# Top-k attention with a low-rank mixer: another order inside the deep steps

## The chip, the cores and the metric

The kernel runs on one core of one Trainium2 chip. What is measured is the device time of one execution in microseconds, from the first to the last instruction of the core. The core has five engines that run side by side and wait for one another by semaphores: PE (TensorE, the matrix multiplier, with its weight loads as PEld), DVE (VectorE), ACT (ScalarE), POOL (GpSimd) and SP (SyncE, which here only issues DMA).

## What is computed

Eight batches of eight heads; 576 rows of 64 channels in each head; all in fp32. Each row of the attention keeps the 32 largest of its 576 scores. The result goes through a mixer along the sequence (rank 32) and an MLP of 512 to 2048 to 512 channels.

```python
def _attn_ref(q, k, v):                      # q, k, v: (8, 8, 576, 64)
    scores = scale * np.matmul(q, k.transpose(0, 1, 3, 2))
    kth = np.partition(scores, -32, axis=-1)[..., -32:-31]
    scores = np.where(scores >= kth, scores, -1e9)
    attn = np.exp(scores - np.max(scores, axis=-1, keepdims=True))
    attn = attn / (np.sum(attn, axis=-1, keepdims=True) + 1e-09)
    return np.matmul(attn, v)

def _moe_ref(x, U, V, w_ch1, w_ch2):         # x: (8, 576, 512)
    h = x.transpose(0, 2, 1) @ U @ V
    u = x + h.transpose(0, 2, 1)
    return u + np.maximum(u @ w_ch1, 0.0) @ w_ch2
```

## The kernel before

Heads are worked on in pairs, 32 pairs `g` in all. A pair has five steps `t`: four with 128 query rows of both heads, and a tail (`t == NT == 4`) with the last 64 rows of each head, side by side in the partitions. Steps are numbered `n = 5 g + t`. The pieces of a step are these.

```python
def scores(g, t):            # PE: 4 fp32 products of 288 columns; ACT: copies to Ssb
    ...
def front(g, t):             # a generator; each next() issues one part
    ...
    for c in order:
        ms[c] = first[:, c]
        nc.vector.max(ms[c], curs[c])            # the first 8 of the 32
    yield
    for i in range(1, TOPK // 8):
        if i == 1:                               # ACT: exp of head 0
            nc.scalar.mul(nmax[:, 0:n], first[:, 0:n, 0], -SCALE)
            ... weigh(chunks[c], Es[c], nmax[:, c : c + 1])
        for c in order: ... nc.vector.match_replace(nxt, ms[c], curs[c], NEG)
        for c in order: ... nc.vector.max(ms[c], curs[c])
        yield
    if pooled:                                   # head 1: masked by POOL
        nc.gpsimd.tensor_scalar(Es[1], chunks[1], ms[1][:, 7:8], NEG, ALU.is_lt, ALU.mult)
        nc.gpsimd.tensor_tensor(chunks[1], chunks[1], Es[1], ALU.add)
    for c in ...: nc.vector.scalar_tensor_tensor(out=Es[c], ...)   # head 0: masked by DVE
    yield
    if pooled:                                   # ACT: exp of head 1, after POOL
        weigh(chunks[1], Es[1], nmax[:, 1:2], sums[1])
    yield

def turns(g, t):             # a generator: E transposed by PE, copied to PT by ACT
    for h in range(nh):      # nh = 2, in the tail 1
        ... 4 transposes; nc.scalar.copy(PT[...], tp)
        yield
    ... 1 transpose (the last columns); nc.scalar.copy
    yield

def values(g, t):            # PE: PT times v
    ...
    if t == NT:
        inverse(g, ...)      # DVE: 1 / (sum + 1e-9) of the whole pair
        ... 5 fp32 products
        nc.scalar.mul(x[half(h), NT, half(h)], O[half(h), half(h)], den[half(h), 2 * NT :])
        return
    ... 9 fp32 products; nc.scalar.copy(XTs[g][:, cols(t)], O)

def mixed(g, wait):          # a generator, advanced by one at each fill()
    ... 4 transposes of XT; nc.scalar.copy(X4, tp4)
    nc.gpsimd.tensor_tensor(X4, X4, den4, ALU.mult)
    for _ in range(wait): yield
    ... 5 products with U; nc.scalar.copy(Tb, pT); yield
    ... two products with V, x added by PE; copies to uT; two yields
    if gi == NPAIR - 1: fillers.append(mlp(b))   # the batch is complete: its MLP may start
```

`mlp(b)` is a generator too: 256 fp32 products of 320 and then 256 of 256 columns, one per `next`, with the relu on ACT and, at the end of an output block, an addition on POOL and a transposition by PE (`turned_back`). `fill()` puts a fixed share of it between the pieces of attention:

```python
SLOTS, SHORT, EARLY = 8, 0.65, 0.91
share = MLP_WORK / (NPAIR * SLOTS * (NT + SHORT))
def fill(k=1):
    ...
    if mixing and next(mixing[0], True): mixing.pop(0)
    due += share * (SHORT if t == NT else 1) * (EARLY if n <= 2 * ALONE + 2 else 1)
    while due > 0: ... due -= next(fillers[0], None)
```

The first batch (`n < ALONE == 20`) has no MLP beside it and an order of its own. From step 21 on, the deep steps, each step issues the pieces in this order:

```python
fill()
next(turning, None)              # E of step n-2, head 1
fill()
next(turning, None)              # E of step n-2, last columns
fill()
next(ready, None)                # transposes of the next pair's q, k
fill()
if n - 2 >= ALONE:
    values(*divmod(n - 2, CH))
if n + 1 < STEPS:
    scores(*divmod(n + 1, CH))
next(here, None)                 # here is front(n): exp of head 0, second 8
next_params(1)                   # decodes a slab of weights while there are any
if n - 2 >= ALONE and (n - 2) % CH == NT:
    mixing.append(mixed((n - 2) // CH, 4))
fill()
next(here, None)                 # third 8
fill()
if n <= STEPS:
    turning = turns(*divmod(n - 1, CH))
next(turning, None)              # E of step n-1, head 0
fill()
next(here, None)                 # fourth 8
next(last, None)                 # last is front(n-1): exp of head 1
if t in (1, 3):
    next_params(1)
next(here, None)                 # masking
fill()
```

Of the kernel before, what the change touches and what calls it, by code (L numbers as in the profile page):

```python
# [24 lines left out]
def kernel(  # L25
# [35 lines left out]
    NT, TAIL = 4, 64  # L61
# [53 lines left out]
    def rows(t):  # L115
        return P if t < NT else TAIL

    def cols(t):
        return slice(t * P, t * P + rows(t))
# [4 lines left out]
    def half(h):  # L124
        return slice(h * D, (h + 1) * D)
# [139 lines left out]
    def scores(g, t):  # L265


        qkT = qkTs[g]
        n = rows(t)
        S2 = attn.tile([P, 2 * (S + TAIL)], F32, tag="Ssb", name="Ssb", bufs=3)  # L270
        scs = [ps_s.tile([P, 2, 512], F32, tag="sc", name="sc") for _ in range(2)]
        for i, sc in enumerate(scs):
            for h in range(2):
                nc.tensor.matmul(  # L274
                    sc[slice(0, n) if t < NT else half(h), h, 0:HALF],
                    lhsT=qkT[half(h), 0, cols(t)],
                    rhs=qkT[half(h), 1, i * HALF : (i + 1) * HALF],
                    start=True,
                    stop=True,
                )  # L280
        if t == NT:
            for i, sc in enumerate(scs):
                for h in range(2):
                    nc.scalar.copy(
                        S2[half(h), i * HALF : (i + 1) * HALF], sc[half(h), h, 0:HALF]
                    )
            S2s[g, t] = [S2[:, 0:S]]
            return

        main = S2.rearrange("p (h n) -> p h n", h=2)  # L290
        last = S2[:, MAIN : MAIN + 2 * TAIL].rearrange("p (h n) -> p h n", h=2)
        copy = nc.vector.tensor_copy if g + t == 0 else nc.scalar.copy
        copy(main[:, :, 0:HALF], scs[0][:, :, 0:HALF])  # L293
        nc.scalar.copy(main[:, :, HALF:MAIN], scs[1][:, :, 0 : MAIN - HALF])
        nc.scalar.copy(last, scs[1][:, :, MAIN - HALF : HALF])  # L295
        S2s[g, t] = [S2[:, 0:S], S2[:, S : 2 * S]]
# [59 lines left out]
    def turns(g, t):  # L356


        E2 = probs.pop((g, t))
        nh = 2 if t < NT else 1  # L360
        PT = attn.tile([P, 2 * NT + 1, P], F32, tag="PT", name="PT")
        PTs[g, t] = PT
        for h in range(nh):
            tp = ps_t.tile([P, NT, P], F32, tag="tp", name="tp")
            for j in range(NT):
                a = h * (S + TAIL) + j * P
                nc.tensor.transpose(tp[:, j, :], E2[:, a : a + P], ident)  # L367
            nc.scalar.copy(PT[:, NT * h : NT * h + NT], tp)  # L368
            yield
        tp = ps_t.tile([P, P], F32, tag="tp", name="tp")  # L370
        a = MAIN if nh == 2 else S - P
        nc.tensor.transpose(tp, E2[:, a : a + P], ident)  # L372
        nc.scalar.copy(PT[:, NT * nh], tp)
        yield
# [6 lines left out]
    def values(g, t):  # L381

        PT = PTs.pop((g, t))
        va, vd, vt = (a[g % NV] for a in (vas, vds, vts))
        O = ps_t.tile([P, P], F32, tag="tp", name="O")
        if t == NT:
            den, x = dens[g], xs[g % 2]
            inverse(g, 2 * NT if g == NPAIR - 1 else 0, 2 * NT + 1)
            for j in range(NT + 1):
                nc.tensor.matmul(  # L390
                    O,
                    lhsT=PT[:, j],
                    rhs=va[:, :, j, :] if j < NT else vt,
                    start=(j == 0),
                    stop=(j == NT),
                )
            for h in range(2):
                nc.scalar.mul(x[half(h), NT, half(h)], O[half(h), half(h)], den[half(h), 2 * NT :])
            return
        nc.tensor.matmul(O, lhsT=vd, rhs=PT[:, 2 * NT], start=True, stop=False)  # L400
        for j in range(NT):
            for h in range(2):
                nc.tensor.matmul(  # L403
                    O[half(h)],
                    lhsT=va[:, h, j, :],
                    rhs=PT[:, NT * h + j],
                    start=False,
                    stop=(j == NT - 1),
                )
        if t == 0:  # L410
            XTs[g] = attn.tile([P, MAIN], F32, tag="XT", name="XT")
        nc.scalar.copy(XTs[g][:, cols(t)], O)  # L412
# [124 lines left out]
    CH = NT + 1  # L537
    STEPS = NP * CH
    ALONE = NPAIR * CH


    SLOTS, SHORT, EARLY = 8, 0.65, 0.91
    share = MLP_WORK / (NPAIR * SLOTS * (NT + SHORT))
    fillers, mixing, due = [], [], 0.0

    def fill(k=1):

        nonlocal due
        for _ in range(k):
            if mixing and next(mixing[0], True):  # L550
                mixing.pop(0)
            due += share * (SHORT if t == NT else 1) * (EARLY if n <= 2 * ALONE + 2 else 1)
            while due > 0:
                if not fillers:
                    due = 0.0
                    break
                done = next(fillers[0], None)
                if done is None:
                    fillers.pop(0)
                else:  # L560
                    due -= done
# [3 lines left out]
    t = 0  # L565
# [3 lines left out]
    turning = ready = iter(())  # L569
    fronts = {}  # L570
    for n in range(STEPS + 2):
        g, t = divmod(n, CH)
        if n < STEPS:
            if t == 0 and g + 1 < NP:
                load(g + 1)
            if t == 1 and g + 1 < NP:
                ready = prep(g + 1)
            fronts[n] = front(g, t)
            next(fronts[n])
        here, last = fronts.get(n, iter(())), fronts.pop(n - 1, iter(()))  # L580
        if n >= ALONE - 1 and n <= ALONE:

            list(turning)
            if n < ALONE:
                scores(*divmod(n + 1, CH))
            list(turns(*divmod(n - 1, CH)))
            if n < ALONE:
                values(*divmod(n - 2, CH))
                next(here)
            values(*divmod(n - 1, CH))  # L590
            if n < ALONE:
                inverse(g, 0, 2 * NT)
                next(here)
                mixing.append(mixed(g, 1))
                fill()
                next(here)
                next(here)
                continue
            fill()
            scores(*divmod(n + 1, CH))  # L600
            next(here)
            while mixing:
# [3 lines that stand above are left out]
            next(last, None)  # L606
            next(here)
            fill()
            next(here)
            next(here)  # L610
            fill()
            continue
        if n < ALONE:
            next(turning, None)
            next(turning, None)
            scores(*divmod(n + 1, CH))
            fill()
            if n >= 1:
                turning = turns(*divmod(n - 1, CH))
            if n >= 2:  # L620
                values(*divmod(n - 2, CH))
            next(here)
            next_params(1)
            next(turning, None)
            fill()
            next(last, None)
            next(ready, None)
            next(here)
            fill()
            if n >= 2 and (n - 2) % CH == NT:  # L630
                mixing.append(mixed((n - 2) // CH, 3))
            next(here)
            if t == 1:
                next_params(1)
            next(here)
            fill()
            continue
        fill()
        next(turning, None)
        fill()  # L640
        next(turning, None)
        fill()
        next(ready, None)
        fill()
        if n - 2 >= ALONE:
            values(*divmod(n - 2, CH))
        if n + 1 < STEPS:
            scores(*divmod(n + 1, CH))
        next(here, None)
        next_params(1)  # L650
        if n - 2 >= ALONE and (n - 2) % CH == NT:
            mixing.append(mixed((n - 2) // CH, 4))
        fill()
        next(here, None)
        fill()
        if n <= STEPS:
            turning = turns(*divmod(n - 1, CH))
        next(turning, None)
        fill()
        next(here, None)  # L660
        next(last, None)
        if t in (1, 3):
            next_params(1)
        next(here, None)
        fill()
# [33 lines left out]
```

## Time and profile before

| | |
|---|---|
| median of 3 runs | 1861.4 us (1859.79 to 1863.52) |
| span of the profiled run | 1861.6 us |
| PE busy | 1750.6 us, 94% |
| PEld busy | 1324.0 us, 71% |
| DVE busy | 1617.2 us, 87% |
| ACT busy | 1008.1 us, 54% |
| POOL busy | 635.7 us, 34% |
| mean granted clock of TensorE | 0.966 |

A line such as `L472` is a line of the kernel's text. L367 and L372 are the transposes of E, L274 the scores, L390, L400 and L403 the values, L424 to L449 the mixing, L472 and L491 the two halves of the MLP, L519 the turn-back. L320, L330 and L334 are the top-k search on DVE, L337 and L338 the masking on POOL, L340 that on DVE, and L300 the Exp on ACT. An fp32 product is two instructions on PE, so the profile counts twice the products of the program; a transpose is one. An engine's list of waits tells whom it waited for, how long in total, how often, and the longest one. In a timeline, what stands in brackets at a line's end is the idle time before it and the instruction that ended it.

### The profile page before, as it was taken

To read this page: it belongs to the slowest core of one execution; us is meant where nothing else is said; L and a number is where in the kernel's file an instruction comes from. 1 tells how busy PE (TensorE), PEld (TensorE's weight loads), DVE (VectorE), ACT (ScalarE), POOL (GpSimd) and SP (SyncE) were. 2 spreads that over 40 slices of the span, in tenths; PEclk is the share of its full clock that TensorE was granted. 3 is DMA by queue.
4 is the path that set the end of the run, shared out by engine and by line. 5 is a ranking of instruction groups with operands and counts; after the bars stand their busy time and mean duration, and the time that the engine had idled before them with its cause. 6 is when DMAs were issued, how large, how long until landed. Compare 5 with 4: busy or idle time off the path is not lost.

```text
span 1861.6 us, 29241 instructions
## 1 busy us (share of the span) xinstructions
PE 1750.6 (94%) x10528; PEld 1324.0 (71%) x10528; DVE 1617.2 (87%) x3316; ACT 1008.1 (54%) x2466; POOL 635.7 (34%) x432
## 2 busy tenths in 40 slices
PE   4565789999999999999999999999999999999999
PEld 3443556787777877788777877788777877788677
DVE  7999999999999999999999999999999999996000
ACT  4666677555655555555555555555555555554111
POOL 4556466433333332323233332332323332322000
PEclk7677799999999999999999999999999999999999
DMA  3222222101000010110001010101001010000000
GB/s 98 76 72 75 63 81 81 28 23 32 15 21 22 23 29 21 30 25 24 23 13 31 21 32 20 28 22 27 14 24 27 25 30 21 10 8 7 6 14 12
DMA packets 127296, 58.23 MB, mean 31 GB/s; under 512 B 89904, under 2 KB 124976, under 8 KB 127152
## 3 DMA queue, kind: packets, MB, share of 16 engines
q1 hardware_dynamic: 126096, 56.10, 11.3%
q8 instruction: 84, 1.38, 0.3%
q14 instruction: 60, 0.49, 0.1%
q10 hardware_dynamic: 1056, 0.26, 0.1%
HBM read 46.89 MB, written 9.44 MB: 30 GB/s over the span
## 4 chain that ended last, share of the span: by engine, by line
PE 84%; DVE 10%; ACT 4%; issue 1%; POOL 1%; DMA 0%; POOLq 0%; SPq 0%; DVEq 0%; ACTq 0%
PE mm L472 27%; PE mm L491 26%; PE sc L274 9%; PE O L403 6%; PE tp L367 6%; DVE rr L330 4%; DVE m L334 3%; PE O L390 2%; PE up L447 2%; PE O L400 1%; DVE first L320 1%; PE tp L254 1%; PE tp L519 1%; PE up L449 1%; PE tp L372 1%
## 5 line engine op out<-in xcount | busy, mean ns | idle before, releaser
L334 DVE MAX8 m<-rr 128x8 f32<-128x576 f32 x864 | 614.8, 749 | 5.5
L491 PE MATMUL mm<-hT,w 128*128 128x256 f32 (+1 forms) x2048 | 562.2, 410 | 0.0
L472 PE MATMUL mm<-uT,w 128*128 128x256 f32 (+1 forms) x2048 | 557.9, 411 | 1.5 <-ACT hT L484 1.5
L337 POOL TENSOR_SCALAR E<-Ssb,m 128x576 f32<-128x576 f32 x127 | 285.2, 2246 | 650.7 <-DVE m L334 512.7
L472 PEld LDWEIGHTS mm<-uT,w 128*128 128x128 f32 x2048 | 363.3, 190 | 108.6 <-issue 27.6
L491 PEld LDWEIGHTS mm<-hT,w 128*128 128x128 f32 x2048 | 360.5, 190 | 97.7 <-issue 22.5
L330 DVE MATCH_REPLACE8 rr<-m,rr 128x576 f32<-128x576 f32 x576 | 427.8, 743 | 0.0
L367 PE MATMUL tp<-ident,E 128*128 128x128 f32 x1152 | 184.7, 285 | 53.8 <-ACT E L300 38.7
L368 ACT COPY PT<-tp 128x512 f32<-128x512 f32 x288 | 168.4, 585 | 114.9 <-PE tp L367 113.0
L300 ACT ACTIVATE E<-Ssb,nmax 128x576 f32<-128x576 f32 x288 | 223.8, 778 | 5.9 <-POOL Ssb L338 0.7
L367 PEld LDWEIGHTS tp<-ident,E 128*128 128x128 f32 x1152 | 144.9, 147 | 106.9 <-ACT E L300 50.7
L274 PE MATMUL sc<-qkT 64*128 64x288 f32 (+1 forms) x1280 | 212.5, 454 | 0.3 <-ACT Ssb L293 0.3
L330 DVE MATCH_REPLACE8 rr<-first,Ssb 128x576 f32<-128x576 f32 x288 | 211.8, 742 | 0.0
L320 DVE MAX8 first<-Ssb 128x8 f32<-128x576 f32 x288 | 205.4, 750 | 0.9 <-ACT Ssb L295 0.9
L340 DVE SCALAR_TENSOR_TENSOR E<-Ssb,m,E 128x576 f32<-128x576 f32 x161 | 137.8, 856 | 65.6 <-ACT E L300 48.2
L338 POOL TENSOR_TENSOR Ssb<-Ssb,E 128x576 f32<-128x576 f32 x127 | 178.9, 1408 | 10.6
L484 ACT ACTIVATE hT<-mm 128x320 f32<-128x320 f32 (+1 forms) x256 | 104.4, 408 | 119.8 <-PE mm L472 119.0
L412 ACT COPY XT<-O 128x128 f32<-128x128 f32 x128 | 34.0, 266 | 215.1 <-PE O L403 215.1
L403 PE MATMUL O<-PT,va 128*64 128x128 f32 x2048 | 147.7, 289 | 0.0
L274 PEld LDWEIGHTS sc<-qkT 64*128 64x128 f32 (+1 forms) x1280 | 110.2, 187 | 51.7 <-issue 25.4
L504 DVE TENSOR_TENSOR oT<-uT,mm 128x320 f32<-128x320 f32 (+1 forms) x8 | 3.6, 455 | 146.6 <-PE mm L491 146.6
L403 PEld LDWEIGHTS O<-PT,va 128*64 128x64 f32 x2048 | 116.0, 143 | 16.8 <-issue 2.9
(73 smaller groups left out, 1484.3 us busy)
## 6 DMA issues: line engine op xcount, KB each, us to landing
raw<-in_moe_w_ch_dram SPq DMA_DIRECT2D x32, 512.0 KB, 3.7
va<-in_v_dram SPq DMA_DIRECT2D x64, 128.0 KB, 2.5
out_dram<-ob SPq DMA_DIRECT2D x64, 128.0 KB, 1.9
ld_q<-in_q_dram SPq DMA_DIRECT2D x63, 128.0 KB, 2.8
ld_k<-in_k_dram SPq DMA_DIRECT2D x63, 128.0 KB, 2.8
ld_ends<-in_q_dram SPq DMA_DIRECT2D x32, 32.0 KB, 2.2
ld_ends<-in_k_dram SPq DMA_DIRECT2D x32, 32.0 KB, 2.2
vd<-in_v_dram SPq DMA_DIRECT2D x64, 16.0 KB, 2.0
```

The lines of the kernel that those rows point to most:

```text
L274: nc.tensor.matmul(sc[slice(0, n) if t < NT else half(h), h, 0:HALF], lhsT=qkT[half(h), 0, cols(t)], rhs=qkT[half(h), 1, i * HALF : (i + 1 ...
L300: nc.scalar.activation(E, chunk, AF.Exp, bias=nmax, scale=SCALE, accum_out=total)
L320: nc.vector.max(ms[c], curs[c])
L330: nc.vector.match_replace(nxt, ms[c], curs[c], NEG)
L334: nc.vector.max(ms[c], curs[c])
L337: nc.gpsimd.tensor_scalar(Es[1], chunks[1], ms[1][:, 7:8], NEG, ALU.is_lt, ALU.mult)
L338: nc.gpsimd.tensor_tensor(chunks[1], chunks[1], Es[1], ALU.add)
L367: nc.tensor.transpose(tp[:, j, :], E2[:, a : a + P], ident)
L368: nc.scalar.copy(PT[:, NT * h : NT * h + NT], tp)
L403: nc.tensor.matmul(O[half(h)], lhsT=va[:, h, j, :], rhs=PT[:, NT * h + j], start=False, stop=(j == NT - 1),)
L472: nc.tensor.matmul(ph[:, 0:w], lhsT=w1[:, cc, f * P : (f + 1) * P], rhs=uT[:, cc, lo:hi], start=(cc == 0), stop=(cc == NC - 1),)
L491: nc.tensor.matmul(po[:, 0:w], lhsT=w2[:, f, c * P : (c + 1) * P], rhs=hTs[f][:, 0:w], start=(f == 0), stop=(f == NF - 1),)
```

## The change

Inside a deep step the values of two steps back and the scores of the next step come first. All of E of the step before is then transposed within the step, where before its second half was left to the following one. After a tail (`t == 0`) the tail's values follow in the same step, and with them the mixing of the pair, one step sooner than before and with three fills instead of four ahead of the product with U. The share of the first MLP in a fill (`EARLY`) is raised and its range is shortened by a step, since the second batch is mixed a step sooner. The decoding of weights moves toward the step's end.

```diff
-    SLOTS, SHORT, EARLY = 8, 0.65, 0.91
+    SLOTS, SHORT, EARLY = 8, 0.65, 0.955
...
-            due += share * (SHORT if t == NT else 1) * (EARLY if n <= 2 * ALONE + 2 else 1)
+            due += share * (SHORT if t == NT else 1) * (EARLY if n <= 2 * ALONE + 1 else 1)
...
-        fill()
-        next(turning, None)
-        fill()
-        next(turning, None)
-        fill()
-        next(ready, None)
-        fill()
-        if n - 2 >= ALONE:
+        if n - 2 >= ALONE and t != 1:
             values(*divmod(n - 2, CH))
         if n + 1 < STEPS:
             scores(*divmod(n + 1, CH))
+        fill()
+        turning = turns(*divmod(n - 1, CH)) if n <= STEPS else iter(())
+        next(turning, None)
+        fill()
+        next(here, None)
+        if t == 0:
+            next(turning, None)
+        fill()
+        next(last, None)
+        next(ready, None)
+        fill()
+        next(here, None)
+        if t == 0:
+            values(*divmod(n - 1, CH))
+            mixing.append(mixed((n - 1) // CH, 3))
+        fill()
+        next(turning, None)
+        fill()
+        next(turning, None)
         next(here, None)
         next_params(1)
-        if n - 2 >= ALONE and (n - 2) % CH == NT:
-            mixing.append(mixed((n - 2) // CH, 4))
-        fill()
-        next(here, None)
-        fill()
-        if n <= STEPS:
-            turning = turns(*divmod(n - 1, CH))
-        next(turning, None)
-        fill()
-        next(here, None)
-        next(last, None)
+        fill()
         if t in (1, 3):
             next_params(1)
         next(here, None)
         fill()
```

More of the change, by code (lines that the diff above doesn't have):

```diff
@@ L637 @@
             continue
+        if n - 2 >= ALONE and t != 1:
+            values(*divmod(n - 2, CH))
+        if n + 1 < STEPS:
+            scores(*divmod(n + 1, CH))
+        fill()
[13 more added lines that the diff above has]
+            mixing.append(mixed((n - 1) // CH, 3))
         fill()
@@ L641 @@
         next(turning, None)
-        fill()
-        next(ready, None)
-        fill()
-        if n - 2 >= ALONE:
-            values(*divmod(n - 2, CH))
-        if n + 1 < STEPS:
-            scores(*divmod(n + 1, CH))
         next(here, None)
         next_params(1)
-        if n - 2 >= ALONE and (n - 2) % CH == NT:
-            mixing.append(mixed((n - 2) // CH, 4))
         fill()
-        next(here, None)
-        fill()
-        if n <= STEPS:
-            turning = turns(*divmod(n - 1, CH))
-        next(turning, None)
-        fill()
-        next(here, None)
-        next(last, None)
         if t in (1, 3):
```

## The prediction

> **What bounds the kernel now.** I read the page's slices first, then a table of stretches, then PE's and DVE's waits in the deep steps (the name the change gives to the steps from 21 on, in which the MLP of one batch runs on TensorE between the attention steps of the next).
>
> ```profile
> PE   4565789999999999999999999999999999999999
> DVE  7999999999999999999999999999999999996000
> PEclk7677799999999999999999999999999999999999
> ```
>
> Each digit is 46.5 us. DVE (the top-k search) is full from the start until about 1700 us; PE fills up only near 300 us and stays full to the end. The stretches say it in figures (the columns after the length are PE, PEld, DVE, ACT and POOL busy, then clock and DMA):
>
> ```profile
> 200.00:300.00 100.00, 87.94 (x502) 60.00 (x501) 95.91 (x203) 70.87 (x160) 53.88 (x37) 0.92 0.25 74
> 300.00:360.00 60.00, 57.79 (x360) 41.31 (x358) 57.67 (x118) 35.51 (x86) 36.33 (x25) 1.00 0.18 47
> 360.00:400.00 40.00, 40.00 (x259) 32.74 (x256) 38.99 (x79) 25.39 (x65) 10.84 (x6) 1.00 0.09 22
> 450.00:500.00 50.00, 46.42 (x274) 33.29 (x273) 46.52 (x95) 27.71 (x68) 14.97 (x10) 0.97 0.05 13
> 900.00:1000.00 100.00, 100.00 (x597) 71.81 (x596) 94.33 (x193) 56.83 (x140) 33.01 (x21) 1.00 0.09 22
> ```
>
> From 500 us on PE has no room: 99 to 100 of every 100 us. DVE still has 5 or 6. [...] I checked with start-to-start times in the chain of work that ended last:
>
> ```profile
> 581.75 1.92 PE mm L472 x8
> 794.11 1.92 PE mm L472 x8
> 1006.48 1.92 PE mm L472 x8
> ```
>
> The same piece comes back every 212.36 us, one batch. In the last stretch, which is MLP alone, 128 instructions of 320 columns take 34.46 us, 0.269 us each; in a deep step the timeline has eight in 2.15 us from start to start, also 0.269. So mixing attention into the MLP costs PE nothing: it is packed. What PE and DVE wait for between 450 and 1650 us, first PE's list, then DVE's:
>
> ```profile
> PE tp L519 <- POOL oT L507: 7.1, 6, 2.9
> PE tp L519 <- ACT x L428: 0.7, 1, 0.7
> ```
>
> ```profile
> DVE E L340 <- ACT E L300: 43.8, 34, 2.2
> ```
>
> PE waits 7.8 us in 1200. DVE waits 43.8 us there, for the Exp that ACT issues behind the copies of PE's scores: DVE is held by PE, not PE by DVE. All that an order can win after 21 steps is therefore PE's idle time, which I collect below.
>
> [...] Here the weight loads are busy 72 to 80% of a deep stretch, so by that alone some room would be left; the start-to-start times above show none, and I follow them. [...] this trace has 269 ns for each of the two instructions of an fp32 product[...], and 269 is used. [...] the Exp of ACT at 322.36 us had its input from POOL since 315.7, but ran behind three activations of the weight decoding (319.47 to 321.4) and behind copies. [...] here 2.9 us of idling at 457.5 is followed by slow matmuls, shown next.
>
> **The change part by part.** It adds and removes no instruction; PE's work is the same to the matmul. Three things move.
>
> (1) *The handover from the first MLP to the second.* Before, the first MLP runs out while the second's input has just been made, and the last turn-back waits for POOL, which is in a 2.22 us masking operation:
>
> ```profile
> 456.90 0.60 PE L491 MATMUL mm<-hT,w 128*128 128x256 f32 x2
> 460.41 0.44 PE L519 MATMUL tp<-ident,oT 128*128 128x128 f32 x2 [2.91 <-POOL oT L507]
> 460.68 0.60 PE L254 MATMUL tp<-ident,ld_k 128*128 128x128 f32 x4
> 461.12 1.68 PE L472 MATMUL mm<-uT,w 128*128 128x320 f32 x4
> 462.59 0.64 PE L400 MATMUL O<-PT,vd 128*128 128x128 f32 x2
> 463.15 1.98 PE L403 MATMUL O<-PT,va 128*64 128x128 f32 x16
> ```
>
> The hole costs 2.91 us, and the slow clock after it 0.44 (1.68 for four where 1.24 is usual) + 0.26 (0.64 for 0.38) + 0.89 (1.98 for 1.09) = 1.6, together 4.5 us. At the later handovers the two matmuls are followed by the qkT transposes and only then by the turn-back; PE waits 0.84 us there ((7.1 - 2.91) / 5). In the changed program the tail's values and the mixing come a step sooner, EARLY is raised to match, and the first handover has that same form (three matmuls, four transposes, turn-back). So 4.5 - 0.8 = 3.7 us are saved. The other five handovers keep their form, and their 0.84 us.
>
> (2) *The first deep steps, 230 to 325 us.* Here DVE is the full engine and PE has holes of 0.2 to 1.8 us in the timeline, 8.3 us together, mostly for the Exp (L300), twice for relu (L484), all behind ACT's decoding of weights. Counted in program order, both kernels have put the same 56.6 us of MLP ahead of the scores of step 31 (105 matmuls of 0.539 us), so I compare the time at which those scores start: 335.75 us before. In the changed order E of step 28 is transposed within step 29. POOL must first do two weight joins (2 x 2.65 us), now just before that step's masking, and then the mask (3.63 us): DVE ends step 28 near 322.5, POOL near 330.5, the Exp at 331.3, then 2.2 us of PE work to the step's end and 1.25 of values put the scores at about 334.8. Saved: about 1 us, and since ACT's two decodings now come 0.8 us apart (4.2 us in one burst) that may as well be minus 2.
>
> (3) *The steady steps.* Work per batch is the same 212.4 us of PE. The question is whether the shorter way from DVE to PE makes holes. Take a step of the changed order with PE's start at 0: values 1.25, scores 1.17, fill 0.84 (124 us of MLP per batch, over 4 x 8 x 4.65 fills, is 0.83), so the first transposes of E come at 3.3 and need the masking of the step before; the Exp comes after the scores' copies and the first transposes at 5 to 5.8, and DVE's masking ends at 6.6 or later. A full step lasts PE 10 to 12 us, so DVE may be as early as 3.4 to 5.4 us before the next step's start and as late as 3.3 after it (2.5 where POOL's half is asked for). That is a play of 6 us, as wide as before (there the transposes lie 1.7 us behind the scores instead of 0.8, but half of E waits a further step). DVE needs about 51.0 us for the five steps of a pair (4 x 10.9, 6.2, and 1.2 for the reciprocals) where PE needs 53.1, so it sits at the early end of the play: no holes. The tight spot is the step after a tail. There the reciprocal must be ready for the tail's values: DVE reaches it at 12.3 - 3.8 = 8.5 us after the tail's masking, which is 7.2 to 7.3 us in the step; PE's values end at 7.4. And the mixing's X goes through ACT (0.56 us) and POOL (1.04 us) to the U product: at the end of the old run this chain takes 2.56 us from the first transpose at 1720.00 to POOL's end at 1722.56, with ACT free. The old order leaves 4.1 to 4.5 us for it (0.44 and six matmuls and transposes of E); the new leaves 0.44 + 2.6 = 3.0 us. Margins of 0.2 and 0.4 us: now and then ACT, with a relu in its way, will overrun them. I allow an overrun of 0.15 us in every second pair, 2 us over 28 pairs.
>
> (4) *The end.* The last MLP starts when the last batch is mixed, one step sooner in program order, but the rest of the MLP before it fills the chain on both sides, and PE is full. Zero.
>
> Sum: -3.7 - 1 + 2 = -2.7; 1861.4 - 2.7 = **1858.7 us**.
>
> **The rivals.** *The handover and the start pay in full and no margin breaks*: -3.7 and most of the 8.3 us of early holes, about 1851. For it: EARLY is set anew to fit, and the MLP ahead of the scores of step 46 is 146.3 us instead of 142.5, so 3.8 us more has been put into the time that DVE sets. Against: PE has no holes from 325 to 457, so more work there only moves what follows. *The tail step becomes a wait*: ACT, in order, stands at the multiplication by the reciprocal, or PE at the U product, 0.5 to 1 us per pair, 14 to 28 us in all: about 1872 to 1885. For it: the margins under (3), and the U product (L435) already waited for POOL 10.5 us in four early steps of the old run. Against: DVE's and ACT's idle shares. *DVE becomes the bound in the deep steps*: this would need PE under 51 us a pair; its work is fixed at 53.1, so it is out unless DVE itself is stopped by a late Exp.
>
> **Range and chances.** Nothing in reach is 2%, 37 us: PE's idle time after step 21 is under 20 us in all, and a loss of 37 would need 1.3 us of new wait in each of 28 pairs. Eight times in ten between 1849 (the first rival) and 1869 (0.4 us a pair). Faster by over 2%: 0.01; within 2%: 0.97; slower: 0.02.
>
> **What would show it.** Right: the repeat length of a batch stays 212.0 to 212.8 us; the hole of 2.9 us and the slow values near 460 us are gone, with 0.8 us at every handover; the waits of DVE for the Exp remain. Wrong: PE waits for POOL x (L429) at L435 or for ACT at L390/L424 in steady pairs; ACT waiting for DVE den (L379) by more than 10 us in all; a batch that lasts over 214 us; or scores of step 31 later than 338 us.

## The result, and the profile after

1879.9 us (median of 5 runs, 1879.66 to 1882.15) against 1861.4: a ratio of 1.0103, 95% interval 1.0088 to 1.0118. The change makes the kernel 18.5 us slower; 1858.7 was predicted, in a range up to 1869.

The page's slices after, to be held against those before:

```profile
PE   4565789999999999999999999999999999999999
DVE  7999999999999999999899998999899989997000
PEclk7677899999999999999999999999999999999999
```

PE looks the same; DVE has 8s where there were only 9s. The same stretches as before (PE, PEld, DVE, ACT, POOL busy, clock, DMA):

```profile
300.00:360.00 60.00, 54.68 (x313) 38.52 (x312) 55.56 (x113) 36.68 (x85) 38.20 (x26) 0.94 0.16 47
450.00:500.00 50.00, 48.65 (x303) 35.71 (x303) 45.38 (x93) 27.58 (x69) 16.78 (x11) 1.00 0.10 25
900.00:1000.00 100.00, 99.30 (x591) 70.66 (x588) 90.32 (x188) 56.46 (x140) 31.02 (x20) 1.00 0.08 20
```

From 300 to 360 us PE has lost 3.1 us, and its clock fell to 0.94; from 450 to 500 it has gained 2.2; in a steady stretch it is still at 99.3, so a change of the steady steps hardly shows in busy time. It shows in the chain, where one piece returned every 212.36 us before, and now:

```profile
686.97 2.16 PE mm L472 x8
901.95 2.16 PE mm L472 x8
```

That is 214.98 us a batch, 2.6 more. The waits between 450 and 1650 us, PE's and then DVE's:

```profile
PE tp L367 <- ACT E L300: 7.4, 22, 0.5
PE tp L519 <- POOL oT L507: 7.1, 6, 1.4
```

```profile
DVE E L340 <- ACT E L300: 75.4, 30, 3.7
```

New is PE's wait for the Exp ahead of the transposes of E, 22 times, once in each pair. PE's wait for the turn-back has the same sum as before, but other parts: 0.84 us at the first handover instead of 2.91, and 0.89 to 1.35 instead of 0.83 at the five later ones. DVE waits 31.6 us more than before; it is held by PE more than before, not less.

To place the loss I took the start of each step's scores (L274) from PE's timelines of both kernels:

| scores of step | before, us | after, us | difference |
|---|---|---|---|
| 21 | 228.09 | 225.86 | -2.23 |
| 23 | 249.19 | 242.60 | -6.59 |
| 24 | 259.87 | 259.96 | +0.09 |
| 29 | 316.11 | 314.37 | -1.74 |
| 31 | 335.75 | 341.07 | +5.32 |
| 42 | 446.46 | 456.15 | +9.69 |
| 43 | 465.06 | 469.57 | +4.51 |
| 54 | 580.56 | 586.65 | +6.09 |
| 154 | 1642.38 | 1661.09 | +18.71 |
| 159 | 1693.96 | 1713.50 | +19.54 |
| end | 1861.6 | 1877.9 | +16.3 |

Up to step 20 the kernels are the same, and profiled runs pass step 21 up to 2.6 us apart; only differences from there on are used (from -2.23 to +16.3 at the end they are the 18.5 us of the medians). Two losses last: about 7 us between steps 29 and 31, and 12.6 us between 54 and 154, 0.63 in each of 20 pairs. A third loss, of 6.7 us between steps 23 and 24, only takes back what stood gained before; part of that gain was work put off, as PE has ten MLP instructions fewer between steps 21 and 23 than before. (An MLP is 512 instructions on PE, 2560 in the five batches between steps 54 and 154. So it is 128 fp32 products of 320 columns and then 128 of 256, half of the numbers given with the kernel before.) The handover (42 to 43) gives back 5.2. At the end 3.2 come back because less MLP is left; between 31 and 42 about 2.6 of the 4.4 us are that same MLP, done early, and 1.0 is the first part of a mixing (L424, L435) that came behind the scores of step 42 before. So 1.0 of the handover's 5.2 us is moved work as well, and about 4.2 are time saved.

**The loss at the start**, in the timelines of POOL, ACT and PE:

```profile
324.31 1.36 POOL L172 TENSOR_TENSOR w<-w,raw 128x512 uint32<-128x512 uint32 x1 [4.17 <-ACT w L161]
325.76 1.70 POOL L174 TENSOR_TENSOR w<-w,raw 128x512 uint32<-128x512 uint32 x1
327.42 1.29 POOL L172 TENSOR_TENSOR w<-w,raw 128x512 uint32<-128x512 uint32 x1
328.79 1.29 POOL L174 TENSOR_TENSOR w<-w,raw 128x512 uint32<-128x512 uint32 x1
330.06 2.21 POOL L337 TENSOR_SCALAR E<-Ssb,m 128x576 f32<-128x576 f32 x1
332.35 1.44 POOL L338 TENSOR_TENSOR Ssb<-Ssb,E 128x576 f32<-128x576 f32 x1
```

```profile
333.83 0.78 ACT L300 ACTIVATE E<-Ssb,nmax 128x576 f32<-128x576 f32 x1 [3.77 <-POOL Ssb L338]
```

```profile
327.98 2.32 PE L491 MATMUL mm<-hT,w 128*128 128x320 f32 x8
334.75 1.11 PE L367 MATMUL tp<-ident,E 128*128 128x128 f32 x4 [4.45 <-ACT E L300]
335.65 1.27 PE L491 MATMUL mm<-hT,w 128*128 128x320 f32 x2
336.72 0.42 PE L372 MATMUL tp<-ident,E 128*128 128x128 f32 x1
336.93 2.34 PE L491 MATMUL mm<-hT,w 128*128 128x320 f32 x4
339.07 0.64 PE L400 MATMUL O<-PT,vd 128*128 128x128 f32 x2
339.63 1.51 PE L403 MATMUL O<-PT,va 128*64 128x128 f32 x16
341.07 1.24 PE L274 MATMUL sc<-qkT 64*128 64x288 f32 x8
```

POOL joins two slabs of weights before it masks; ACT stands 3.77 us before the Exp; PE stops for 4.45, and then runs slowly: from 334.75 to 341.07, where the granted clock was 0.54, it does in 6.32 us what at the usual rates takes 3.5. The loss between steps 23 and 24 has the same form. POOL joins two slabs from 243.80 us and masks only at 249.53, PE stops, and runs at a clock of 0.51 afterwards (255.44 to 258.63 us):

```profile
254.18 0.66 PE L367 MATMUL tp<-ident,E 128*128 128x128 f32 x4 [4.03 <-ACT E L300]
```

**The loss in the steady steps**, PE and then ACT in one tail step:

```profile
920.70 1.24 PE L274 MATMUL sc<-qkT 64*128 64x288 f32 x8
921.87 0.81 PE L472 MATMUL mm<-uT,w 128*128 128x320 f32 x2
922.51 0.60 PE L367 MATMUL tp<-ident,E 128*128 128x128 f32 x4
922.95 2.32 PE L472 MATMUL mm<-uT,w 128*128 128x320 f32 x8
925.78 0.66 PE L367 MATMUL tp<-ident,E 128*128 128x128 f32 x4 [0.51 <-ACT E L300]
```

```profile
921.55 0.64 ACT L293 COPY Ssb<-sc 128x576 f32<-128x576 f32 x1 [0.47 <-PE sc L274]
922.09 0.54 ACT L294 COPY Ssb<-sc 128x448 f32<-128x448 f32 x1
922.51 0.28 ACT L295 COPY Ssb<-sc 128x128 f32<-128x128 f32 x1
923.15 0.59 ACT L368 COPY PT<-tp 128x512 f32<-128x512 f32 x1 [0.35 <-PE tp L367]
923.63 0.21 ACT L325 ACTIVATE nmax<-first 128x1 f32<-128x1 f32 x1
923.87 0.78 ACT L300 ACTIVATE E<-Ssb,nmax 128x576 f32<-128x576 f32 x1
924.55 0.42 ACT L484 ACTIVATE hT<-mm 128x320 f32<-128x320 f32 x1
924.87 0.77 ACT L300 ACTIVATE E<-Ssb,nmax 128x576 f32<-128x576 f32 x1
```

In a tail step the fills are short (a factor of 0.65). PE is ready for the transposes of head 1 at 922.95 + 8 x 0.269 = 925.10, 4.4 us after the scores began; ACT has copies, a copy of E, the tail's own Exp and a relu in its row, and ends the Exp of head 1 at 925.6.

### The profile page after: what moved, and what is told of

Same layout as the page of the kernel before. It is cut to its first block, busy times and chain, and to the rows that moved or that the text cites. A ratio compares the mean times of both kernels' runs of the same rounds, so it can differ in the third digit from the quotient of the medians.

```text
span 1877.9 us, 29166 instructions
## 1 busy us (share of the span) xinstructions
PE 1752.8 (93%) x10528; PEld 1320.0 (70%) x10528; DVE 1598.4 (85%) x3316; ACT 1003.5 (53%) x2466; POOL 637.2 (34%) x432
## 4 chain that ended last, share of the span: by engine, by line
PE 79%; DVE 10%; ACT 5%; issue 3%; POOL 3%; DMA 0%; POOLq 0%; DVEq 0%; SPq 0%; ACTq 0%
PE mm L472 25%; PE mm L491 23%; PE sc L274 8%; PE tp L367 6%; PE O L403 6%; DVE rr L330 4%; DVE m L334 3%; ACT E L300 3%; PE O L390 2%; PE up L447 2%; PE O L400 1%; DVE first L320 1%; PE tp L254 1%; DVE E L340 1%; PE tp L519 1%
## 5 line engine op out<-in xcount | busy, mean ns | idle before, releaser
L300 ACT ACTIVATE E<-Ssb,nmax 128x576 f32<-128x576 f32 x288 | 216.2, 772 | 18.8 <-POOL Ssb L338 13.6
L274 PE MATMUL sc<-qkT 64*128 64x288 f32 (+1 forms) x1280 | 212.8, 454 | 0.0
L507 POOL TENSOR_TENSOR oT<-oT,uT 128x320 f32<-128x320 f32 (+1 forms) x56 | 47.6, 850 | 318.0 <-ACT oT L506 318.0
L429 POOL TENSOR_TENSOR x<-x,den 128x512 f32<-128x512 f32 x32 | 33.4, 1044 | 348.6 <-ACT x L428 284.7
L274 PEld LDWEIGHTS sc<-qkT 64*128 64x128 f32 (+1 forms) x1280 | 110.3, 187 | 58.0 <-issue 35.0
```

Source lines behind the costliest of these rows:

```text
L274: nc.tensor.matmul(sc[slice(0, n) if t < NT else half(h), h, 0:HALF], lhsT=qkT[half(h), 0, cols(t)], rhs=qkT[half(h), 1, i * HALF : (i + 1 ...
L300: nc.scalar.activation(E, chunk, AF.Exp, bias=nmax, scale=SCALE, accum_out=total)
```

## The experiments

All times are medians with the ratio to the kernel before, which was run beside them, and its 95% interval. A batch is the distance between the scores of steps 54 and 154, divided by five: 212.36 us before, 214.89 after.

### e1: the first decoding early again

```diff
+        next_params(1)             # behind the step's first next(here)
...
-        next_params(1)             # behind the step's third next(here)
```

> The changed kernel, with the first decoding of a weight slab back behind the Exp of head 0 instead of near the step's end. Theory (the start): in steps 21 to 30 POOL joins the decoded weights ahead of the masking, so the Exp of head 1 is late, ACT stands before it, and PE idles (12.3 us for the Exp between 231 and 345 us, against 4.9 before). Then 6 to 9 us come back: 1871 to 1874 us, while a batch in the steady steps still lasts 215.0 us. Rival: the 7 us lost between the scores of steps 29 and 34 come from the raised EARLY or from transposing E a step sooner, which this leaves in: within 2 us of 1880.

1875.8 us, 1.0077 (1.0062 to 1.0092); batch 214.88. Four come back, not six to nine: in steps 1 and 3 of a pair the second decoding still lands before the masking. PE's longest wait for the Exp between 231 and 470 us falls from 4.4 to 2.4. The direction fits, the size is a miss.

### e2: both decodings behind the masking

```diff
-        next_params(1)
         fill()
-        if t in (1, 3):
-            next_params(1)
         next(here, None)           # masking
+        next_params(1)
+        if t in (1, 3):
+            next_params(1)
```

> The changed kernel, with both decodings moved behind the step's masking, so that POOL masks first and joins weights afterwards, while ACT's burst of decoding stays at the step's end and DVE still shifts bits between two steps. If the order on POOL is the cause of the loss at the start, 4 to 8 us come back (1872 to 1876 us) and PE's longest wait for the Exp before 345 us falls from 4.4 to under 2. If the burst on ACT, or DVE's wait for it (3.6 us), is the cause, little comes back: 1878 to 1882 us.

1871.7 us, 1.0055 (1.004 to 1.007); batch 214.97. The scores of step 31 start at 330.1 us instead of 341.1. POOL now masks first:

```profile
320.86 2.31 POOL L337 TENSOR_SCALAR E<-Ssb,m 128x576 f32<-128x576 f32 x1 [4.78 <-DVE m L334]
323.25 1.46 POOL L338 TENSOR_TENSOR Ssb<-Ssb,E 128x576 f32<-128x576 f32 x1
324.67 1.29 POOL L172 TENSOR_TENSOR w<-w,raw 128x512 uint32<-128x512 uint32 x1
```

The amount of decoding is the same and so is its burst on ACT, and the long stops at the start are gone: PE's longest wait for the Exp before 345 us falls from 4.4 us to 0.8. But not only POOL's order was changed. On DVE, too, the shift of the decoded bits (L171) now comes behind the masking, and DVE's wait of 3.6 us for ACT's decoding is gone with it. For step 28 the trace parts the two. POOL begins this masking 9.2 us sooner (330.06 us in the change, 320.86 here). DVE's last MAX8 pair of the search, first in the change and then here, begins 2.5 us sooner:

```profile
322.44 1.41 DVE L334 MAX8 m<-rr 128x8 f32<-128x576 f32 x2
319.94 1.41 DVE L334 MAX8 m<-rr 128x8 f32<-128x576 f32 x2
```

The other 6.7 us are the joins that stood ahead, with their short wait for the shift. No run changes POOL's order alone, so what each of the two is worth in time is not shown.

Of the 11 us at step 31, 7.2 are left at step 42. The rest is lost between 31 and 33: PE stops at the product with U for POOL's multiplication of X and runs slowly afterwards (clock 0.66 from 341 to 346 us).

```profile
341.40 0.62 PE L435 MATMUL pT<-x,U 128*32 128x128 f32 x10 [2.06 <-POOL x L429]
```

POOL waited there for ACT, and ACT 4.47 us for DVE's reciprocal: here it is DVE that sets the pace.

### e3: the Exp of head 1 first, in the tail step

```diff
+        if t == NT:
+            next(last, None)       # Exp of head 1 of the step before
         next(here, None)           # Exp of the tail
...
-        next(last, None)
+        if t != NT:
+            next(last, None)
```

> The changed kernel, with ACT's Exp of head 1 of the step before issued ahead of the tail's own Exp in the tail step alone. Theory (the steady steps): in the tail step the fills are short, and ACT's row of copies, copy, Exp of the tail, relu, Exp of head 1 takes 5.0 us from the scores while PE is at the transposes of head 1 after 4.5; PE then waits 0.3 to 0.5 us in each pair. With the Exp taken first the wait goes: a batch lasts 213.2 to 213.9 instead of 215.0 us, in all 6 to 10 us less, 1870 to 1874 us. Rival (the second one of the prediction: the sooner values of the tail and the mixing take the time): no change, 1878 to 1882 us, and a batch stays at 215.0.

1866.5 us, 1.0026 (1.0017 to 1.0035); a batch is back at 212.36, the old value, and PE's waits from 450 to 1650 us are one line:

```profile
PE tp L519 <- POOL oT L507: 5.5, 6, 1.2
```

13.4 us come back, more than expected from 7.4 us of recorded waiting (more on that at the end). This one move, of head 1's Exp ahead of the tail's and a fill sooner, takes all of the steady loss away; e10 tells its two parts apart.

### e4: the kernel before with EARLY 0.90

```diff
-    SLOTS, SHORT, EARLY = 8, 0.65, 0.91
+    SLOTS, SHORT, EARLY = 8, 0.65, 0.90
```

> The kernel before, with EARLY 0.90 instead of 0.91 and nothing else. The handover from one MLP to the next then falls behind the next values and scores, 2.4 us later than the last block's addition on POOL. Theory: the hole of 2.9 us and the slow clock behind it (4.5 us) and the five waits of 0.84 us go: 1852 to 1856 us. Rival: the work that is not done early only moves to the end, and the hole with it: 1860 to 1863 us.

1875.6 us, 1.007 (1.0053 to 1.0087), a clear miss of mine. The hole at 460 us went (4.9 us gained between the scores of steps 42 and 43), but the later batches became 3.3 us longer on average, 215.66:

```profile
672.63 0.70 PE L491 MATMUL mm<-hT,w 128*128 128x256 f32 x2
675.99 0.44 PE L519 MATMUL tp<-ident,oT 128*128 128x128 f32 x2 [2.65 <-POOL oT L507]
```

The block's last product now comes behind the scores and the turn-back directly behind it, so no work lies between. ACT's copy of the block stands in its row behind the copies of those scores and an Exp, at 674.38 us, and POOL, idle until then, adds at 674.81. I had taken the block for finished before the scores; and it is ACT's row, not POOL's masking as the next expectation still has it, that makes this wait. The stop is 2.65 us at all five later handovers, but what it costs is not the same: at three of them PE goes on at a granted clock of 1.00 and a batch takes 214.7 us; at 890.7 and 1108.4 us the granted clock is 0.50 and 0.63 in the 4 us behind the turn-back, and the batch takes 217.7 and 216.4.

### e5: the kernel before, the last block turned back inside the next MLP

```diff
+    late = []                      # shared by all batches
     def mlp(b):
-        late = []
...
-        late.pop()()
+        if b == B - 1:
+            late.pop()()
```

> The kernel before, with the last output block of an MLP turned back inside the next MLP (after its fourth block of the first product) instead of at once, for all batches but the last. The previous run of EARLY 0.90 showed that the handover's wait is for POOL, which masks first; this takes the wait away whatever POOL does. Expected: no wait of PE for POOL oT (L507) at a handover; the hole of 2.9 us at 460 and its slow clock gone (4.5 us) and five waits of 0.84 us that count 1.0 us each from start to start, together 9 to 10 us: 1851 to 1853 us. If the hole at 460 is a lack of input for the second MLP and not the wait for POOL, only the five waits go: 1855 to 1857 us.

1849.6 us, 0.9941 (0.9926 to 0.9956), a little more than expected; a batch is 211.32 and PE has no recorded wait at all between 500 and 1640 us. The hole at 460 us was the wait for the turn-back, not a lack of input.

### e6 and e7: the cures together

e6 is the change with e2 and e3; e7 has the edit of e5 as well.

> The changed kernel with both cures: decoding behind the masking, and the Exp of head 1 ahead of the tail's Exp in the tail step. If the two losses are separate, their returns add: 1879.9 - 8.2 - 13.4 = 1858.3 us, 3 us under the kernel before, a batch of 212.4 us. If both hang on the same wait (ACT behind POOL's masking), the sum is smaller: 1862 to 1866 us.

1855.9 us, 0.9979 (0.9968 to 0.999); batch 212.36. 24.0 us come back, slightly more than the 21.6 of the single returns together: two separate losses.

> The same two cures and the last output block turned back inside the next MLP. The handovers' waits in the changed order are 0.8 to 1.4 us, counting 1.0 to 1.6: six of them are 7 us. Expected 1850 to 1853 us, a batch of 211.2 us. If DVE becomes the bound once PE's holes are gone (DVE's waits for the Exp are then under 20 us between 500 and 1640), it stays above 1855.

1846.7 us, 0.9926 (0.9911 to 0.994), better than expected; batch 211.20. The fastest version of this study, 2.9 us under e5. DVE still waits 39.3 us for the Exp between 500 and 1640, so PE is still the bound, at its work alone.

### e8: the mixing back in the step t = 1

```diff
-        if n - 2 >= ALONE and t != 1:
+        if n - 2 >= ALONE:
             values(*divmod(n - 2, CH))
...
-        if t == 0:
-            values(*divmod(n - 1, CH))
-            mixing.append(mixed((n - 1) // CH, 3))
+        if t == 1 and n - 2 >= ALONE:
+            mixing.append(mixed((n - 2) // CH, 3))
```

with e3, and EARLY with its range as before.

> The changed kernel with the Exp of head 1 first in the tail step (1866.5 us), and with the tail's values and the mixing back in the step t = 1, EARLY and its range as before. It tells what the sooner mixing is worth by itself. Theory: nothing in the steady steps, as PE has the same work: a batch stays within 0.5 us of 212.4; the first handover is again a turn-back with little behind the last product, so it may wait 1 to 3 us more: 1866 to 1871 us. Rival: the sooner mixing is a gain of its own (or a loss): a batch over 213 or under 211.9.

1871.2 us, 1.0057 (1.0042 to 1.0072); batch 212.52, so mixing sooner is worth nothing in the steady steps. Against e3, PE has 6.5 us less MLP to do ahead of the scores of step 159 (counted in program order) and reaches them only 3.1 us sooner. Of the 3.4 us that are missing, part is lost at the handover: steps 42 to 44 take 2.6 us longer, but 1.0 of this is the first part of the mixing (L424, L435), which in e3 lies before step 42, and so about 1.5 us are new waiting, with PE held 1.35 us for a copy of ACT (L256) and 1.26 instead of 0.83 us for the turn-back. Where the rest goes stays open. What the sooner mixing is seen to be good for is the handover.

### e9 and e10: two other handles on the tail step

e9 is the change with SHORT 0.90 for 0.65; e10 issues `next(last)` of the tail step directly behind `next(here)`, a fill sooner but not ahead of the tail's Exp.

> The changed kernel with SHORT 0.90 instead of 0.65: the fills of the tail step are longer (0.83 units instead of 0.63) and all others 5% shorter; no order is changed. If the steady loss is PE coming too early to head 1's transposes in the tail step because the fills there are short, five fills bring it there 0.9 us later and the wait goes without touching ACT: a batch of 212.4 to 212.9 instead of 214.9 us, 1866 to 1870 us in all. If the order of the two Exp costs by itself, whatever the fills: 1878 to 1882 us.

1869.4 us, 1.0045 (1.0029 to 1.0062); PE's wait for the Exp is gone from 500 to 1640 us. The batch of 213.05 is a little over the expected, as the handovers' waits are 1.64 us each here; in e3 they are about 0.9.

> The changed kernel with the Exp of head 1 in the tail step issued directly behind the tail's Exp, one fill sooner than in the change but not ahead of the tail's Exp. ACT then leaves out one relu (0.32 us) of its row. The stop is 0.68 us from start to start at 925 us, so about half of it goes: a batch of 213.4 to 214.0 us, 1872 to 1875 us. If being one fill sooner were what helped in the run with the Exp of head 1 first, the batch falls to 212.4 us as there.

1876.6 us, 1.0085 (1.007 to 1.01); batch 214.29. Only 0.15 us a pair comes back, half of what I expected. In the change the stops are of two kinds: 0.45 to 0.51 us where a relu stands between the two Exps in ACT's row (as at 925 us), and 0.19 in every second pair, where none does. Here all 22 are 0.19, against 0.33 on average. So being sooner is not enough; the tail's Exp must be out of the way, or PE later (e9).

## Why the prediction was wrong

Two of the signs that were named for being wrong came: a batch of over 214 us (214.89) and scores of step 31 later than 338 us (341.07).

**What bounds the kernel**: right. PE's work stayed the bound, and DVE's waits for the Exp remain (75.4 us). Two readings were slightly off: the weight loads are busy 67 to 82% of the deep stretches of the table, not 72 to 80, and PE did have one hole between 325 and 457 us, the 0.7 us in the list of waits.

**(1) The handover**: right for the first one. "3.7 us are saved"; about 4.2 were (of the 5.2 us between steps 42 and 43), and its turn-back waits 0.84 us. "The other five handovers keep their form, and their 0.84 us" was wrong: four of them wait 1.35 us now.

**(2) The first deep steps**: failed at "Saved: about 1 us". The mechanism was named, weight joins ahead of the masking, but the size was off: the scores of step 31 were put at 334.8 us and came at 341.1. POOL ended its masking at 333.8 instead of 330.5, 3.3 us late, mostly because DVE's search ended late: DVE ended step 28 at 326.3 instead of 322.5. By then it had waited 3.6 us in all for ACT's decoding, which I had not counted. (Its masking also took 1.86 us instead of 0.82, but POOL's joins had begun before it.) The slow clock after the stop (4.45 us, then 0.54 until 341.07), which I had counted at the handover, I left out here: 2.8 us. With the two terms, 3.3 + 2.8, the scores come at 340.9. e2, which takes the joins and DVE's wait away together, gives back 8.2 us.

**(3) The steady steps**: failed at "no holes", at "The tight spot is the step after a tail" and so at the allowance of 2 us. That DVE sits early was right, as its waits show; the holes came from ACT. I worked out the play for a full step and then looked for the tight place in the step after the tail. None of the waits that I had named came: no wait of PE for POOL x in the steady pairs, none of ACT for the reciprocal. (At the start they do come once the stops are gone: in e6 PE waits 4.1 us for POOL x and ACT 6.8 us for the reciprocal before 345 us.) The tight place was the tail step itself. There the fills are 0.65, so PE is early; the length of ACT's row hardly shrinks with them. In a full step (scores at 952.16 us) ACT ends head 1's Exp 5.2 us after the scores begin and PE transposes head 1 after 6.5; in a tail step ACT ends it after 4.9 and PE is there after 4.4. I had the row of ACT in hand for the first Exp and did not carry it on to the second. In place of 2 us it cost 13.4 (e3), 0.6 in a pair.

**(4) The end**: zero was wrong by 3.2 us of less MLP left, which only returns what was done early.

With both losses taken away the new order gains 4.3 us (e6, 1855.9), close to the 2.7 predicted; it is about what the handover alone saves. The second rival's 1872 to 1885 us held the result, but by luck: its wait of 0.5 to 1 us a pair was to come in another step and for another cause.

## What to carry to other kernels

Where work is given out in steps of unequal length, check the order in the shortest step: the other engines' rows of instructions need not get shorter with the filler (from the full to the tail step ACT's went from 5.2 to 4.9 us, PE's from 6.5 to 4.4). When work is moved closer to what produces it, follow every engine in between, in the order of its own timeline, to the last instruction that the consumer needs, with what now stands ahead of it: in the tail step at 921 us four copies, the tail's Exp and a relu stood ahead of head 1's Exp on ACT, and PE waited 0.51 us. And a wait between two large pieces of work is better removed by putting work of the next piece between than by tuning shares: e5 needed three lines, while a change of EARLY by 0.01 cost 14 us (e4).

## What was not expected of the hardware

A stop of PE cost more here than the idle time that the profile records. At 925 us 0.51 us is recorded, but from start to start PE loses 925.78 - 925.10 = 0.68: the recorded end of the matmuls before, 922.95 + 2.32 = 925.27, lies 0.17 us beyond the 925.10 that 0.269 us from start to start gives; and the four transposes behind the stop take 0.49 instead of 0.44. A stop recorded with 0.19 us (in the change at 548.45) adds the same 0.22: from start to start PE loses 0.36, and 0.05 in the transposes. Over all pairs this gives 0.33 + 0.22 = 0.55 us, and the turn-backs' longer waits (7.1 us against 5.5 in e3) are another 0.08 us a pair: together the 0.63 that a pair is longer. For e10 the same sum, 0.19 + 0.22 + 0.08, gives 0.49, and 0.48 was measured. So halving the recorded wait did not halve the loss.

In these runs the length of a stop did not by itself tell whether PE ran slowly afterwards. The stop of 2.65 us in e4 was followed by a clock of 1.00 three times and of 0.50 and 0.63 in the other two cases; the one of 2.06 us in e2 by 0.66, and the one of 2.91 us at 460 us in the kernel before by 0.65 (460.40 to 465.00 us). What decides it was not tested.
